# A long convolution beside a gated MLP on one core: the inverse transform's turn on VectorE in place of a trip through DRAM, with a new written order

## The chip, the cores and the metric

The kernel runs on one core of one Trainium2 chip. The metric is the device time in microseconds (us) of one execution; lower is better. Times of several runs are given as a median with the lowest and the highest. The profile is that of one more execution, whose own time and span are given beside the median.

## The reference: what is computed

With `xn = layernorm(A_q)` over 640 columns and 2048 rows, the output is the sum of three parts:

```python
kv  = causal_4_tap_filter(A_k, A_shift_k) * A_v          # per column, along the rows
y   = irfft(rfft(kv, 4096) * rfft(A_ssm_k, 4096))[:2048] # a long causal convolution per column
A   = xn * (bf16(y) + kv * A_ssm_D)
h   = sigmoid(xn @ B_w_gate) * (xn @ B_w_up)             # 640 -> 1728
B   = h @ B_w_down                                       # 1728 -> 640
out = A_q + A + B
```

All inputs and the output are bf16.

## The kernel before, in words

**Layout.** Row 16p + b of the sequence lies on partition p, block b (16 blocks). `x` and `xn` are [128, 16, 640] tiles in SBUF; the results are added into `x`, which is stored at the end.

**The MLP** goes in four row tiles t of 512 rows (four blocks each). `gate_mm` and `up_mm` (both through `product`, L293) make one 128-wide slice of the hidden layer with five matmuls each; ScalarE takes the sigmoid (`gate_ev`, L302) and VectorE multiplies (`up_ev`, L308). `down_mm` (L334), `pair_mm` (L341) and `rest_mm` (L351) go back to 640 columns and VectorE adds the sums into `x` (`down_ev` L345, `rest_ev` L356).

**The convolution** goes in five chunks c of 128 columns. Each is a transform in two steps, a product, and an inverse in two steps:

- `kv_op` (16 letters `k` for each chunk; L384 to L393, VectorE): the four taps and the product with v. `h_turn` (`H`, L370, VectorE) turns the filter by 32x32 transposes; it reads with a step of 32 bytes and writes densely.
- `st1_mm` (`a`, L409 and L411, TensorE): the first step, a sum over the 128 partitions. `st1_ev` (`A`, or `I` when VectorE copies it instead of ScalarE) evicts it to the tile `t1`; `wr1` (`w`, L423) writes `t1` to a DRAM buffer and `rd2` (`r`, L433) reads it back in another order.
- `st2_mm` (`b`, L443), `st2_ev` (`B`, or `F` for VectorE), `prod` (`p`: a shuffle at L456 and a product at L458, VectorE).
- `inv1_mm` (`c`, L472), twice for each chunk (y = 2c and 2c+1). Its output has, on each quarter of 32 partitions, 32 indices (h, b), and along the free dimension 16 indices r times 128 columns. `inv1_ev` (`C` on ScalarE, L256, or `J` on VectorE, L259; two 128x1024 halves for each y) evicts it to the tile `ao`.
- **The turn.** The second inverse step needs r on the partitions and (h, b) along the free dimension. In the kernel before, `wr2` (`W`, L488 or L492) writes `ao` to the DRAM buffer `d2`, and two `rdb` (`R`, L502) for each chunk read it back as `bi` in the other order. These DMAs are issued by SyncE (SP), each behind whatever SP waits for ahead of it.
- `inv2_mm` (`d`, L511), `inv2_q` (`q`, L516: times `xn`) and `inv2_x` (every other `q`, L521: into `x`).

In the profile all copies by ScalarE stand at L256 and all copies by VectorE at L259; the tile's name tells them apart (`t`, `xz`, `ao`, `kx`). Some of `ao` and `bi` lie in the `kx` tiles once those are free.

**The order.** Each engine runs its instructions in the order in which the program lists them. That order is written out by hand as `ORDER`, a string of 824 letters; each letter takes the next step of its chain. `F`, `J` and `I` take a step of `B`, `C` and `A` with VectorE as the copying engine. `TURNS` permutes two of the chains: `m`, the loads at the start, and `o`, the stores at the end. TensorE has psum tiles in two pools: `psC` (two buffers of two banks, for the transforms) and `psG` (four, for the MLP and the second inverse step).

**Stores.** `store` (L359) sends 14 pieces: 512 columns of one or two row blocks, or the last 128 columns of one to four row blocks. SP issues them, except the very last, which ScalarE issues.

Of the kernel before, what the change touches and what calls it, by code (L numbers as in the profile page):

```python
# [10 lines left out]
BF16 = mybir.dt.bfloat16  # L11
F32 = mybir.dt.float32
# [5 lines left out]
DM = 640  # L18
FF = 1728
P = 128  # L20
NB = S // P
NC = DM // P
NFC = 14
NQ = 4
# [13 lines left out]
def _tables():  # L38

    p = np.arange(P)
    k1 = p + 0.25
    s1 = np.zeros((P, NB, 2, P))
    for b in range(NB):
        psi = 2 * np.pi * k1[None, :] * (16 * p + b)[:, None] / 2048.0
        s1[:, b, 0, :] = np.cos(psi)
        s1[:, b, 1, :] = -np.sin(psi)
    tb = s1.transpose(3, 2, 1, 0) / 2048.0  # L50
    th = 2 * np.pi * np.outer(np.arange(NB), np.arange(NB)) / 16.0
    c, s = np.cos(th), np.sin(th)
# [13 lines left out]
def kernel(  # L66
# [14 lines left out]
    nc = tc.nc  # L81
# [3 lines left out]
    outr = out.flatten_outer_dims().rearrange("(p b) d -> p b d", b=NB)  # L85
# [26 lines left out]
    TB = TBt.bitcast(BF16)  # L112
# [3 lines left out]
    x = res.tile([P, NB, DM], BF16, name="x")  # L116
# [16 lines left out]
    sync = nc.sync  # L133
# [222 lines left out]
        nc.vector.tensor_tensor(xs, pds[t, b0][:, b0:b1, :], xs, ALU.add)  # L356

    def store(b0, b1, lo, hi):
        (nc.scalar if b1 == NB and hi == DM else sync).dma_start(outr[:, b0:b1, lo:hi], x[:, b0:b1, lo:hi])  # L359


    def add_D(c):
# [49 lines left out]

    def st1_ev(c, n, copy=act_copy):
        d = chunks[c]
        if n % 2 == 0:
            d[n // 2] = cv.tile([P, 8, 2, P], BF16, name="t1", bufs=2)
        o = 4 * (n % 2)
        copy(out=d[n // 2][:, o:o + 4, :, :].rearrange("p b s c -> p s b c"), in_=pss[n][:, :, :, :])

    def wr1(c, k):  # L420
        h, part = divmod(k, 2)
        d = chunks[c]
        sync.dma_start(d["d1"][:, h, 8 * part:8 * part + 8, :], d[k].rearrange("p b s c -> p b (s c)"))  # L423

    groups = {}
    xz = cv.tile([P, 3, 3, 8, P], BF16, name="xz")
# [34 lines left out]
    def inv1_mm(y):  # L461

        c, y2 = divmod(y, 2)
        d = chunks[c]
        if y2 == 0:
            d["d2"] = dr.tile([32, P, P], BF16, name="d2", bufs=NC)
        d["pa", y] = ps = [psC.tile([P, 2, 512], F32, name="psa", tag="c") for _ in range(2)]
        lo, hi = sorted((2 * y % 3, (2 * y + 1) % 3))
        for i in range(2):
            for q in range(NQ):  # L470
                for g in range(4):
                    nc.tensor.matmul(ps[g // 2][quad(q), g % 2, :], lhsT=SM[quad(g), i, :],  # L472
                                     rhs=xz[quad(g), lo:hi + 1:hi - lo, 1 + i, 2 * q:2 * q + 2, :],
                                     start=(i == 0), stop=(i == 1))

    def inv1_ev(y, n, copy=act_copy):
        d = chunks[y // 2]
        if n == 0:
            d["ao", y] = kxs[1][:, 0:NB, :] if y >= 7 and y % 2 else cv.tile([P, 16, P], BF16, name="ao")[:, :, :]
        dst = d["ao", y].rearrange("p (s g e) c -> p g s (e c)", s=2, g=4)  # L480
        copy(out=dst[:, 2 * n:2 * n + 2, :, :],
                       in_=d["pa", y][n].rearrange("p g (s f) -> p g s f", s=2))

    def wr2(y):
        c, y2 = divmod(y, 2)
        d = chunks[c]
        if 2 * y % 3 < 2:
            sync.dma_start(d["d2"][16 * y2:16 * y2 + 16].rearrange("r p c -> p r c"), d["ao", y])  # L488
            return
        for n in range(2):  # L490
            lo = 16 * y2 + 8 - 8 * n
            sync.dma_start(d["d2"][lo:lo + 8].rearrange("r p c -> p r c"), d["ao", y][:, 8 * n:8 * n + 8, :])  # L492

    def rdb(c, n):

        d = chunks[c]
        if c >= 3 and n == 1:
            bi = kxs[0][:, 0:NB, :].rearrange("p (h b) c -> p h b c", h=2)
        else:
            bi = cv.tile([P, 2, 8, P], BF16, name="bi")[:, :, :, :]  # L500
        src = d["d2"].rearrange("r (q h b) c -> (r q) h (b c)", q=NQ, h=2)
        sync.dma_start(bi.rearrange("p h b c -> p h (b c)"), src[:, :, 1024 * n:1024 * n + 1024])  # L502
        d["bi", n] = bi

    def inv2_mm(c, m):

        bi = chunks[c]["bi", m // 2]
        chunks[c]["pb", m] = ps = psG.tile([P, 4, P], F32, name="psb", tag="g")
        for i in range(4):
            for h in range(2):  # L510
                nc.tensor.matmul(ps[:, i, :], lhsT=TB[:, h, 4 * m + i, :], rhs=bi[:, h, 4 * (m % 2) + i, :],  # L511
                                 start=(h == 0), stop=(h == 1))

    def inv2_q(c, m):
# [63 lines left out]
    def step(k, fn, *args):  # L578
        chains[k].append((fn, args))
# [62 lines left out]
    for c in range(NC):  # L642
        for n in range(2):
            step("H", h_turn, c, n)
        step("D", add_D, c)
        for n in range(8):
            step("a", st1_mm, c, n)
            step("A", st1_ev, c, n)
        for n in range(4):
            step("w", wr1, c, n)  # L650
        for s in range(4 * c, 4 * c + 4):
            step("r", rd2, s)
            step("b", st2_mm, s)
# [9 lines left out]
        for n in range(2):  # L663
# [28 lines left out]
    for b in (0, 4, 8, 12):  # L692
# [2 lines left out]
    step("o", store, NB - 1, NB, 4 * P, DM)  # L695

    ORDER = """
    mmmmgggmssggmuLuLmsggsZgmugmgmLsuuggsmgggsmkLkgkkkumsmgkusmmgkPgmullmlgulHmgsusgmHmuggDgggmkksuskkaA
    kkkanggkkHaTAAegKuHeawmtkegkkekLgugaAuAgkkaADLgguaawAukmgsgAkggTuLksakkkkkggsguuwLPAkmkaAsthgggsKaaH
    HwVAAugukggaamwsskKKrukkkwkkAAklgggauADkksVggTbwlguBgakssglBkkkAuspprgbBgguBkasnkaKKwIggthTuaAkaugAI  # L700
    suggawspHuLLklkVkkAkkawApggakaLsgkkAKkgeemgAceLPuuggrgHuuCCbBrekkwgVFgkgppDlkkaAauKAggwhsulbgtgBBrwk
    suHaAaAggpsbBBpuWgsgkkwVgucggksrpprCCaaWIAsggukalusaIggukAbFggsuBpbBHsgggpugsswDFcunkpKkCRpkrgCrgsaw
    aIguuAdqdbFqVBppggsWbrggBBqlcCpuJksggbqBuBkgpgrsbBggkkkkkuBaaIgeeuppRdqqepaewAdWArwaAgRaarugAIggqwuc
    CggJswqbpBFupggsdqbBpguWqrrBpdqgscCJqugugbFBgppsuRgbBpggsuddqWqBrrscCJRgugbqqppBBWspggsrbrBBggupupdd
    RqcJgsCpgsubFBprggsbBBuggpsqqudcCdgqJbquWpRRBBpggWsgsppuugcCgJdqqqqgqddqgdqqWogqqsggguguRdRuqooodqqq
    qoggudoogoqqodguoqouoqoo
# [38 lines left out]
```

## Time and profile before

| | before |
|---|---|
| median of 3 runs | 236.81 us (236.79 to 237.27) |
| the profiled execution's own time | 238.36 us |
| its span in the trace | 236.5 us |
| TensorE busy | 227.2 us |
| VectorE busy | 202.1 us |
| ScalarE busy | 134.7 us |
| DMA moved | 56.13 MB |

The span runs from the first to the last event of the trace. Busy times are the union of an engine's instructions; TensorE's matmuls are pipelined and their ends are modelled, so a TensorE that is shown as busy can still lose a little between matmuls. A row "a <- b: 5.0, 2, 3.1" of the view of waits says that the engine stood still before a for 5.0 us in all, two times, at most 3.1 us, until b was done.

### The profile page before, as it was taken

How to read it: one execution, taken by the hardware profiler on the slowest of the kernel's cores; microseconds unless marked ns; L12 is line 12 of the kernel's file. 1: busy time of each engine (PE TensorE's matmuls, PEld its weight loads, DVE VectorE, ACT ScalarE, POOL GpSimd, SP SyncE). 2: the span in 40 equal slices, each digit the busy share in tenths (PEclk: the TensorE clock that was granted, in tenths of full speed). 3: DMA queues.
4: the chain of work that ended last, by engine and by line, in shares of the span. 5: the costliest groups of instructions: out<-in, count | busy, mean ns of one | idle time of the engine just before them, and what ended most of it. 6: DMA issues, size and time to landing. Idle time of an engine off the chain costs nothing.

```text
span 236.5 us, 5598 instructions
## 1 busy us (share of the span) xinstructions
PE 227.2 (96%) x2281; PEld 112.0 (47%) x2281; DVE 202.1 (85%) x321; ACT 134.7 (57%) x197; POOL 12.1 (5%) x27
## 2 busy tenths in 40 slices
PE   8999999979999999999999999999999999999990
PEld 2854444436444444447444445445654444445480
DVE  5542983899898989999998999999999999999591
ACT  2458521368886686993976566566365684651000
POOL 4210020000040000020000000000000000000000
PEclk9999999999999999999999999999999999999998
DMA  6999997997999997799999996899999885684775
GB/s 181 305 264 267 256 306 180 236 230 209 231 274 276 301 238 208 140 226 306 282 245 255 298 333 138 219 242 257 247 288 269 224 237 176 173 247 110 222 242 160
DMA packets 98223, 56.13 MB, mean 237 GB/s; under 512 B 56342, under 2 KB 92438, under 8 KB 98070
## 3 DMA queue, kind: packets, MB, share of 16 engines
q1 hardware_dynamic: 97622, 55.42, 89.3%
q8 instruction: 18, 0.29, 0.5%
q10 hardware_dynamic: 576, 0.36, 0.5%
q14 instruction: 7, 0.06, 0.1%
HBM read 35.45 MB, written 18.35 MB: 228 GB/s over the span
## 4 chain that ended last, share of the span: by engine, by line
PE 63%; DVE 15%; SPq 9%; DMA 8%; issue 3%; DVEq 0%
PE pg L293 16%; PE pu L293 16%; PE pd L334 13%; PE pr L351 4%; DMA kx<-in_A_k_dram 4%; PE ps L409 4%; PE ps L411 4%; DMA w<-in_B_w_up_dram 3%; DVE yx L516 3%; PE ps L443 2%; PE psa L472 2%; SPq L185 2%; DVE x L521 2%; SPq L188 2%; DVE xz L458 2%
## 5 line engine op out<-in xcount | busy, mean ns | idle before, releaser
L293 PEld LDWEIGHTS <-w 128*128 128x128 bf16 x500 | 47.0, 98 | 58.1 <-issue 4.8
L293 PE MATMUL pu<-xnT,w 128*128 128x512 bf16 x250 | 62.3, 380 | 0.0
L293 PE MATMUL pg<-xnT,w 128*128 128x512 bf16 x250 | 62.2, 379 | 0.0
L334 PE MATMUL pd<-wd,hT 128*128 128x512 bf16 x208 | 48.4, 379 | 0.3 <-DMA wd<-in_B_w_down_dram 0.2
L308 DVE TENSOR_TENSOR hT<-sig,pu 128x512 bf16<-128x512 bf16 x52 | 35.0, 682 | 12.5 <-PE pu L293 6.8
L302 ACT ACTIVATE sig<-pg 128x512 bf16<-128x512 f32 x52 | 30.9, 601 | 23.8 <-PE pg L293 20.3
L256 ACT CAST xz<-ps 128x1024 bf16<-128x1024 f32 x33 | 32.4, 1017 | 16.8 <-PE ps L443 16.8
L256 ACT CAST t<-ps 128x1024 bf16<-128x1024 f32 x33 | 32.5, 1011 | 16.6 <-PE ps L411 14.7
L334 PEld LDWEIGHTS <-hT 128*128 128x128 bf16 x208 | 19.7, 98 | 24.9 <-issue 2.7
L458 DVE TENSOR_TENSOR xz<-xz 128x2048 bf16<-128x2048 bf16 x20 | 24.4, 1220 | 0.3
L390 DVE TENSOR_TENSOR acc<-acc,tmp 128x1024 bf16<-128x1024 bf16 x30 | 20.7, 689 | 0.6
L388 DVE TENSOR_TENSOR tmp<-kx,sc 128x1024 bf16<-128x1024 bf16 x30 | 20.7, 689 | 0.5
L409 PE MATMUL ps<-kvh,S1t 128*128 128x512 bf16 x40 | 15.2, 379 | 1.2 <-DVE kvh L393 1.2
L411 PE MATMUL ps<-kvh,S1t 128*128 128x512 bf16 x40 | 15.5, 387 | 0.0
L456 DVE STREAM_SHUFFLE xz<-xz 128x512 f32<-128x512 f32 x20 | 14.5, 725 | 0.0
L516 DVE TENSOR_TENSOR yx<-psb,xn 128x512 bf16<-128x512 f32 x20 | 13.7, 685 | 0.7
L351 PE MATMUL pr<-wd,hT 128*128 128x128 bf16 x224 | 14.2, 219 | 0.0
L351 PEld LDWEIGHTS <-hT 128*128 128x128 bf16 x224 | 13.1, 98 | 2.0 <-issue 0.6
L256 ACT CAST ao<-psa 128x1024 bf16<-128x1024 f32 x11 | 10.8, 1013 | 4.0 <-PE psa L472 2.6
L345 DVE TENSOR_TENSOR x<-pd,x 128x512 bf16<-128x512 f32 x16 | 10.6, 683 | 2.9 <-PE pd L341 2.3
L511 PEld LDWEIGHTS <-TBt 128*128 128x128 bf16 x160 | 10.1, 98 | 3.6 <-issue 0.7
L370 DVE STREAM_TRANSPOSE kvh<-hn 128x512 f32<-128x512 f32 x10 | 10.9, 1096 | 0.0
(62 smaller groups left out, 189.3 us busy)
## 6 DMA issues: line engine op xcount, KB each, us to landing
d<-t SPq DMA_DIRECT2D x20, 512.0 KB, 5.2
t<-d SPq DMA_DIRECT2D x20, 512.0 KB, 5.3
bi<-d SPq DMA_DIRECT2D x8, 512.0 KB, 8.6
d<-ao SPq DMA_DIRECT2D x6, 512.0 KB, 5.3
kx<-in_A_k_dram SPq DMA_DIRECT2D x10, 256.0 KB, 5.2
kvh<-in_A_v_dram SPq DMA_DIRECT2D x10, 256.0 KB, 5.4
hn<-in_A_ssm_k_dram SPq DMA_DIRECT2D x20, 128.0 KB, 5.8
x<-in_A_q_dram SPq DMA_DIRECT2D x3, 640.0 KB, 5.4
```

Of the source, the lines that this page charges most:

```text
L256: nc.scalar.copy(out=out, in_=in_)
L293: nc.tensor.matmul(pg[:, :], lhsT=w[:, c, u * UP + fc * P:u * UP + (fc + 1) * P], rhs=xnT[:, :, c, :], start=(c == 0), stop=(c == NC - 1))
L302: nc.scalar.activation(sig[fc][:, :], pgs[0, fc][:, :], ACT.Sigmoid)
L308: nc.vector.tensor_tensor(hT[:, fc, :], sig[fc][:, :], pgs[1, fc][:, :], ALU.mult)
L334: nc.tensor.matmul(pds[bb][:, :], lhsT=hT[:, fc, bb * P:(bb + 1) * P], rhs=wd[:, fc, 0:4 * P], start=(fc == 0), stop=(bb > 1 and fc == NFC ...
L351: nc.tensor.matmul(pds[t, b0][:, bb, :], lhsT=hT[:, fc, bb * P:(bb + 1) * P], rhs=wd[:, fc, 4 * P:DM], start=(fc == 0), stop=(fc == NFC - 1))
L388: nc.vector.tensor_tensor(d["tmp"][:, :, :], kx[:, lo + 3 - m:hi + 3 - m, :], sb(m), ALU.mult)
L390: nc.vector.tensor_tensor(d["acc"][:, :, :], d["acc"][:, :, :], d["tmp"][:, :, :], ALU.add)
L409: nc.tensor.matmul(ps[:, 0, :, :], lhsT=S1[:, h, :], rhs=cin[c]["kvh"][:, 0, 4 * n4:4 * n4 + 4, :], start=True, stop=True)
L411: nc.tensor.matmul(ps[:, 1, :, :], lhsT=S1[:, h, :], rhs=hp[:, 2 * n4:2 * n4 + 2, :, :], start=True, stop=True)
L458: nc.vector.tensor_tensor(z[:, 1:3, :, :], z[:, 0:1, :, :].to_broadcast((P, 2, 8, P)), z[:, 1:3, :, :], ALU.mult)
L516: nc.vector.tensor_tensor(yx[:, :, :], chunks[c]["pb", m][:, :, :], xn[:, 4 * m:4 * m + 4, c * P:(c + 1) * P], ALU.mult)
```

## The change

Four things change together.

1. **The turn.** `wr2`, `rdb` and the buffer `d2` go. Both y of a chunk are evicted to one `ao` of 32 rows by 128 columns, seen as 64 pairs of bf16 (float32). Four `inv_turn` for each chunk (letter `R`, now on VectorE), each over 16 of the 64 pairs, transpose it in place in 32x32 blocks. `inv2_mm` reads `ao` itself. The table `TB` has its rows reordered to fit. For chunk 3 `ao` is the tile `t1`, for chunk 4 the `kx` tiles, which are now one tile.
2. **Who copies.** Of the letters that copy by VectorE, `F` goes from 7 to 3, `I` from 7 to 3 and `J` from 7 to 4; these eleven evictions go to ScalarE.
3. **The order.** `ORDER` and `TURNS` are new throughout. Letters `g`, `s`, `u`, `k`, `H`, `p`, `q` and so on are as many as before. `W` (10) is gone, and `R` is 20 instead of 10.
4. **Stores.** Those of the last 128 columns for row blocks 8 to 11 and 12 to 14 are issued by ScalarE too.

```diff
-    tb = s1.transpose(3, 2, 1, 0) / 2048.0
+    tb = (s1.transpose(3, 2, 1, 0) / 2048.0).reshape(32, NQ, 2, NB, P).transpose(1, 0, 2, 3, 4).reshape(P, 2, NB, P)
...
-    kxs = [res.tile([P, NB + 3, P], BF16, name="kx%d" % i) for i in range(2)]
+    kx2 = res.tile([P, 2, NB + 3, P], BF16, name="kx2")
+    kxs = [kx2[:, i, :, :] for i in range(2)]
+    t1 = res.tile([P, 2, 8, 2, P], BF16, name="t1")
...
-        (nc.scalar if b1 == NB and hi == DM else sync).dma_start(outr[:, b0:b1, lo:hi], x[:, b0:b1, lo:hi])
+        (nc.scalar if b1 > 11 and hi == DM else sync).dma_start(outr[:, b0:b1, lo:hi], x[:, b0:b1, lo:hi])
...
-        if n == 0:
-            d["ao", y] = kxs[1][:, 0:NB, :] if y >= 7 and y % 2 else cv.tile([P, 16, P], BF16, name="ao")[:, :, :]
-        dst = d["ao", y].rearrange("p (s g e) c -> p g s (e c)", s=2, g=4)
+        if n == 0 and y % 2 == 0:
+            if y // 2 < 3:
+                d["ao"] = cv.tile([P, 32, P], BF16, name="ao")[:, :, :]
+            elif y // 2 == 3:
+                d["ao"] = t1.rearrange("p i b s c -> p (i b s) c")
+            else:
+                d["ao"] = kx2.rearrange("p i b c -> p (i b) c")[:, 0:32, :]
+        dst = d["ao"][:, 16 * (y % 2):16 * (y % 2) + 16, :].rearrange("p (s g e) c -> p g s (e c)", s=2, g=4)
...
-    def wr2(y):
...
-    def rdb(c, n):
...
+    def inv_turn(c, n):
+
+        a = chunks[c]["ao"].bitcast(F32).rearrange("p r c -> p c r")[:, 16 * n:16 * n + 16, :]
+        nc.vector.transpose(a, a)
...
-        bi = chunks[c]["bi", m // 2]
+        bi = chunks[c]["ao"].rearrange("p (h b) c -> p h b c", h=2)
...
-            step("W", wr2, y)
-        for n in range(2):
-            step("R", rdb, c, n)
+        for n in range(4):
+            step("R", inv_turn, c, n)
...
-    TURNS = {"m": [0, 1, 21, 7, 2, 23, 9, 4, 5, 15, 6, 10, 18, 12, 13, 14, 8, 22, 17, 11, 20, 16, 25, 24, 26, 19, 3],
-        "o": [3, 6, 1, 7, 4, 5, 2, 9, 10, 8, 0, 12, 11, 13]}
+    TURNS = {"m": [2, 1, 4, 10, 0, 9, 21, 7, 5, 6, 11, 14, 15, 12, 13, 8, 18, 20, 16, 17, 22, 23, 24, 25, 26, 19, 3],
+        "o": [2, 0, 4, 1, 5, 3, 6, 8, 9, 10, 7, 11, 12, 13]}
```

The written order is read off the two strings by counting letters. What the prediction uses:

| letter number in `ORDER` | before | after |
|---|---|---|
| `k` number 1, 8, 9, 16 (chunk 0's taps) | 44, 92, 93, 109 | 12, 64, 72, 96 |
| first and last `R` | 490, 791 | 437, 790 |
| last `p`, last `c`, last `C` or `J` | 755, 759, 762 | 766, 769, 785 |
| first `o` and fifth `o` (stores) | 778, 802 | 758, 778 |

The start of the new string, for the loads: `mZmgsmgugsmkgummgggkkmLsummgggsusLugsmLLmmm...`; its end: `...sooCqggggCRRRqRgoguuoduqgqdqdgodqqgoqoqqouoguoguoo`. In the new `TURNS`, the loads `m` begin with chunk 0's taps, a `w_up` slice, a `w_gate` slice, the first half of chunk 0's k, the `w_gate` slice that came first before, and chunk 0's halo; the second half of chunk 0's k is 11th instead of 20th.

More of the change, by code (lines that the diff above doesn't have):

```diff
@@ L414, in st1_ev @@
         d = chunks[c]
-        if n % 2 == 0:
-            d[n // 2] = cv.tile([P, 8, 2, P], BF16, name="t1", bufs=2)
         o = 4 * (n % 2)
-        copy(out=d[n // 2][:, o:o + 4, :, :].rearrange("p b s c -> p s b c"), in_=pss[n][:, :, :, :])
+        copy(out=t1[:, n // 2 % 2, o:o + 4, :, :].rearrange("p b s c -> p s b c"), in_=pss[n][:, :, :, :])
     def wr1(c, k):
@@ L422, in wr1 @@
         d = chunks[c]
-        sync.dma_start(d["d1"][:, h, 8 * part:8 * part + 8, :], d[k].rearrange("p b s c -> p b (s c)"))
+        sync.dma_start(d["d1"][:, h, 8 * part:8 * part + 8, :], t1[:, k % 2, :, :, :].rearrange("p b s c -> p b (s c)"))
     groups = {}
@@ L464, in inv1_mm @@
         d = chunks[c]
-        if y2 == 0:
-            d["d2"] = dr.tile([32, P, P], BF16, name="d2", bufs=NC)
         d["pa", y] = ps = [psC.tile([P, 2, 512], F32, name="psa", tag="c") for _ in range(2)]
@@ L477, in inv1_ev @@
         d = chunks[y // 2]
-        if n == 0:
-            d["ao", y] = kxs[1][:, 0:NB, :] if y >= 7 and y % 2 else cv.tile([P, 16, P], BF16, name="ao")[:, :, :]
-        dst = d["ao", y].rearrange("p (s g e) c -> p g s (e c)", s=2, g=4)
+        if n == 0 and y % 2 == 0:
[6 more added lines that the diff above has]
+        dst = d["ao"][:, 16 * (y % 2):16 * (y % 2) + 16, :].rearrange("p (s g e) c -> p g s (e c)", s=2, g=4)
         copy(out=dst[:, 2 * n:2 * n + 2, :, :],
                        in_=d["pa", y][n].rearrange("p g (s f) -> p g s f", s=2))
-    def wr2(y):
[L485 to L489, printed above, removed]
-        for n in range(2):
-            lo = 16 * y2 + 8 - 8 * n
-            sync.dma_start(d["d2"][lo:lo + 8].rearrange("r p c -> p r c"), d["ao", y][:, 8 * n:8 * n + 8, :])
-    def rdb(c, n):
[L496 to L503, printed above, removed]
+    def inv_turn(c, n):
+        a = chunks[c]["ao"].bitcast(F32).rearrange("p r c -> p c r")[:, 16 * n:16 * n + 16, :]
+        nc.vector.transpose(a, a)
     def inv2_mm(c, m):
-        bi = chunks[c]["bi", m // 2]
+        bi = chunks[c]["ao"].rearrange("p (h b) c -> p h b c", h=2)
         chunks[c]["pb", m] = ps = psG.tile([P, 4, P], F32, name="psb", tag="g")
@@ L510, in inv2_mm @@
             for h in range(2):
-                nc.tensor.matmul(ps[:, i, :], lhsT=TB[:, h, 4 * m + i, :], rhs=bi[:, h, 4 * (m % 2) + i, :],
+                nc.tensor.matmul(ps[:, i, :], lhsT=TB[:, h, 4 * m + i, :], rhs=bi[:, h, 4 * m + i, :],
                                  start=(h == 0), stop=(h == 1))
@@ L661 @@
                 step("C", inv1_ev, y, n)
-            step("W", wr2, y)
-        for n in range(2):
-            step("R", rdb, c, n)
+        for n in range(4):
+            step("R", inv_turn, c, n)
         for m in range(4):
@@ L697 @@
     ORDER = """
[L698 to L706, printed above, removed]
-    """
-    TURNS = {"m": [0, 1, 21, 7, 2, 23, 9, 4, 5, 15, 6, 10, 18, 12, 13, 14, 8, 22, 17, 11, 20, 16, 25, 24, 26, 19, 3],
-        "o": [3, 6, 1, 7, 4, 5, 2, 9, 10, 8, 0, 12, 11, 13]}
+    mZmgsmgugsmkgummgggkkmLsummgggsusLugsmLLmmmkkggkuggHHsmmkmmsggmkmPuusDmkggggskkkmukgugsmkkalAHakggsA
+    TnmuuaaIltgggglkkksgkkALLlkaawAeuLgAgkmeakwkggukgkkuueeDKagAaTumAggggaLwkkHtsAsAggKkkuakwKgPuahVKskI
+    kugsugAgwmkkaskgrgsAugaAgsgbBTHkBkKVkgwkkkruukwkslggkptaulAaggkknkKVsukksKAwDaArgsakkgAwLHguubggBFss
+    kkaIahgAugwLaTAappgaAukrgkLmasAAkkkgkukegbBwpggeLFVsllHKcCgpHuuteepCgwDaggArubBuBgkkkkkkggkkpaagAAgh
+    usbBBwuggVpHsHapgAaagguAApcssggurCJkRKsuaggkuwawrDAkRkRARaAsggnukkbBBsgpgsubBgrrwudpaqBdddAcqqCCpqqV
+    pggsqubBBqPgsgpbgBBgqspcCCwgrgkruubBBsgsgkkbgBBRrRRRduauplqsdulpAqqraAwgeaAlggaqpppdaeqqdqAAgscCgJbB
+    eggqlFpppbggBBercCuugguuwCrgaAggbrpRsBBRRRggsuugbBgpppBgwsgcusuCJggsppbBdqrduqgguqBprbqspgdqquBBggsc
+    dCppggqrCbsuuggBRRBgRsusbggBRdpsqupgqqdqgBcgCJgsuupprbggqoBsuBpggpodcsudqqosooCqggggCRRRqRgoguuoduqg
+    qdqdgodqqgoqoqqouoguguoo
+    """
+    TURNS = {"m": [2, 1, 4, 10, 0, 9, 21, 7, 5, 6, 11, 14, 15, 12, 13, 8, 18, 20, 16, 17, 22, 23, 24, 25, 26, 19, 3],
+        "o": [2, 0, 4, 1, 5, 3, 6, 8, 9, 10, 7, 11, 12, 13]}
     left = {k: iter([v[i] for i in TURNS.get(k, range(len(v)))]) for k, v in chains.items()}
```

## The prediction

> **What bounds the kernel now.** I read the page first: span, busy times, the slices.
>
> ```profile
> span 236.5 us, 5598 instructions
> ...
> PE 227.2 (96%) x2281; PEld 112.0 (47%) x2281; DVE 202.1 (85%) x321; ACT 134.7 (57%) x197; POOL 12.1 (5%) x27
> ...
> DMA  6999997997999997799999996899999885684775
> ...
> DMA packets 98223, 56.13 MB, mean 237 GB/s; under 512 B 56342, under 2 KB 92438, under 8 KB 98070
> ```
>
> TensorE is busy nearly always, VectorE 85% of the time, and the DMA engines are nearly full. An average does not say who sets the end, so next come the busy times in stretches of 20 us (columns: stretch, then PE, PEld, DVE, ACT, POOL, clock, DMA share, GB/s).
>
> ```profile
> 0.00:20.00 20.00, 18.82 (x148) 10.98 (x149) 8.93 (x25) 10.02 (x19) 4.93 (x16) 1.00 0.97 253
> 20.00:40.00 20.00, 20.00 (x94) 9.11 (x93) 14.65 (x23) 8.67 (x18) 2.16 (x3) 1.00 1.09 263
> 40.00:60.00 20.00, 18.60 (x129) 9.55 (x128) 16.51 (x25) 12.21 (x19) 0.42 (x1) 1.00 0.91 217
> ...
> 100.00:120.00 20.00, 20.00 (x256) 10.17 (x254) 19.73 (x31) 15.40 (x22) 2.02 (x4) 1.00 1.02 257
> ...
> 160.00:180.00 20.00, 20.00 (x278) 11.19 (x275) 19.39 (x32) 10.85 (x13) 0.00 (x0) 1.00 0.95 266
> ...
> 200.00:220.00 20.00, 19.63 (x244) 9.79 (x243) 19.10 (x31) 8.69 (x12) 0.00 (x0) 1.00 0.64 172
> 220.00:237.00 17.00, 10.37 (x115) 6.98 (x112) 8.19 (x16) 0.00 (x0) 0.00 (x0) 0.95 0.67 201
> ```
>
> From 100 us to 220 us VectorE has 19.1 to 19.7 us of every 20. It is as full as TensorE there, and the free time it has lies before 60 us and after 220 us. So an edit that gives VectorE more work is paid for unless that early and late time is used. The third view is the list of waits (total, times, longest).
>
> ```profile
> DVE hT L308 <- PE pu L293: 6.8, 7, 1.5
> ...
> DVE hT L308 <- ACT sig L302: 5.3, 2, 2.6
> ...
> DVE acc L384 <- DMA kx<-in_A_k_dram: 4.2, 1, 4.2
> ...
> DVE x L345 <- PE pd L341: 2.3, 1, 2.3
> ...
> PE idle L539 <- DVE hT L129: 1.2, 1, 1.2
> ...
> PE psb L511 <- DVE yx L516: 0.2, 1, 0.2
> ```
>
> The last row is the only one with `psb`, the second inverse step, and it names VectorE, not `bi`: no engine stands still for the trip through DRAM. It is hidden already. Taking it away shortens no wait that the profile shows; it frees room in the order and on the queue.
>
> **The change part by part.**
>
> *What goes: the trip.* The listing of DMA issues has it:
>
> ```profile
> bi<-d SPq DMA_DIRECT2D x8, 512.0 KB, 8.6
> d<-ao SPq DMA_DIRECT2D x6, 512.0 KB, 5.3
> ...
> d<-ao SPq DMA_DIRECT2D x4, 256.0 KB, 3.7
> ...
> kx<-d SPq DMA_DIRECT2D x2, 512.0 KB, 6.1
> ...
> d<-kx SPq DMA_DIRECT2D x2, 256.0 KB, 4.7
> ...
> d<-kx SPq DMA_DIRECT2D x1, 512.0 KB, 3.8
> ```
>
> Writes: 6 x 512 + 4 x 256 + 2 x 256 + 512 = 5120 KB; reads: 10 x 512 = 5120 KB. That is 10.5 of 56.1 MB, and 23 issues on SP. I cost its going at nothing: other work hid it. What it buys is distance: 5.3 us out and 8.6 us back stood between the last eviction of a chunk and its second step; now it is four turns.
>
> *What comes: 20 turns.* The trace of before has no transpose that writes with a step. The nearest rows:
>
> ```profile
> L456 DVE STREAM_SHUFFLE xz<-xz 128x512 f32<-128x512 f32 x20 | 14.5, 725 | 0.0
> ...
> L370 DVE STREAM_TRANSPOSE kvh<-hn 128x512 f32<-128x512 f32 x10 | 10.9, 1096 | 0.0
> ```
>
> `inv_turn` has the same 128x512 float32 as `h_turn` at L370, 1096 ns, which reads with a step of 32 bytes and writes densely. The new one reads and writes with a step of 256 bytes. Low end: 725 ns, the shuffle of as many elements, dense on both sides. High end: if the 371 ns between these two rows are the price of the stepped reads, and stepped writes cost the same on top, 1467 ns. I take 1096, the same operation, and keep both ends. What counts on a full engine is the distance to the next start:
>
> ```profile
> 67.23 2.10 DVE L370 STREAM_TRANSPOSE kvh<-hn 128x512 f32<-128x512 f32 x2
> 69.26 1.24 DVE L308 TENSOR_TENSOR hT<-sig,pu 128x512 bf16<-128x512 bf16 x2
> ...
> 187.44 1.22 DVE L259 CAST ao<-psa 128x1024 bf16<-128x1024 f32 x1
> 188.58 0.68 DVE L308 TENSOR_TENSOR hT<-sig,pu 128x512 bf16<-128x512 bf16 x1
> ```
>
> Two turns take 69.26 - 67.23 = 2.03 us, 1.015 each, and an eviction by VectorE 1.14 us. So: 20 x 1.015 = 20.3 us come.
>
> The Trainium skill speaks against this edit: "SBUF — State Buffer", in the section on Door 1, says that SBUF has lines of 16 bytes and that each access which crosses to a new line pays a penalty. Here every element of the turn crosses, in reading and in writing; by that page both sides would pay, which is the first rival below. The 1096 beside 725 ns agrees for reads; no run here shows it for writes.
>
> *What moves to ScalarE: eleven evictions* (4 + 4 + 3). VectorE is rid of 11 x 1.14 = 12.5 us. ScalarE gets 11 x 1.01 us by this row:
>
> ```profile
> L256 ACT CAST ao<-psa 128x1024 bf16<-128x1024 f32 x11 | 10.8, 1013 | 4.0 <-PE psa L472 2.6
> ```
>
> That makes 146 us busy of some 235, so it costs nothing as long as nobody waits behind one; if the cover is gone it costs VectorE the waits of rival 2.
>
> VectorE's balance: +20.3 - 12.5 = **+7.8 us**.
>
> *What the order gives back.* Stops of VectorE early and late, and its last instruction:
>
> ```profile
> 12.48 1.28 DVE L308 TENSOR_TENSOR hT<-sig,pu 128x512 bf16<-128x512 bf16 x2 [2.64 <-ACT sig L302]
> ...
> 23.55 0.69 DVE L308 TENSOR_TENSOR hT<-sig,pu 128x512 bf16<-128x512 bf16 x1 [1.47 <-PE pu L293]
> ...
> 41.99 0.69 DVE L384 TENSOR_TENSOR acc<-kx,sc 128x1024 bf16<-128x1024 bf16 x1 [4.20 <-DMA kx<-in_A_k_dram]
> ...
> 222.57 1.29 DVE L345 TENSOR_TENSOR x<-pd,x 128x512 bf16<-128x512 f32 x2 [2.33 <-PE pd L341]
> ...
> 230.81 0.43 DVE L521 TENSOR_TENSOR x<-x,yx 128x512 bf16<-128x512 bf16 x1
> ```
>
> - The 4.2 us stop at 42 us is for the second half of chunk 0's k, the 20th of the loads; it becomes the 11th, and the ninth `k` comes at letter 72. I take all 4.2 us as gone. Between none and 4.2.
> - `up_ev` waits 6.8 + 5.3 us, most of it from 9.8 to 23.6 us, while nothing else lies in VectorE's queue: the first `k` of before is letter 44. It is letter 12 now, and the first half of k is the fourth load. The first 2.6 us stay (no `k` ahead of it); of the other 9.5 I take 4.0 as filled, about six `kv_op`. Bounds: none and 9.5. In exchange one gate slice lands after k; TensorE, without a stop there now, may lose up to 1 us, which I leave in the range.
> - The stop of 2.3 us at 220 us waits for TensorE. With VectorE the fuller engine at the end, TensorE will be ahead: gone.
>
> Given back: 4.2 + 4.0 + 2.3 = 10.5 us.
>
> *New waits.* A turn must wait for the last `inv1_ev` of its chunk. For chunk 4 the last `C` is the letter right before the first `R`: `prod`, then `inv1_mm`, then two ScalarE evictions of 1.01 us, with about 1.5 us of VectorE work beside them. I put 1.3 us there; behind the waiting turn stand the last `u` and `q`, the whole end. 0.7 us for the other four chunks, whose `R` stand at least five letters behind their last `C`. Reuse of `ao`, `t1` and `kx`: nothing, since the last `wr1` of a half of `t1` is issued tens of letters ahead.
>
> VectorE's last instruction ends at 231.24 + 7.8 - 10.5 + 2.0 = **230.5 us**.
>
> *The end: stores.*
>
> ```profile
> SPq L359 <- DVE x L521: 9.1, 2, 5.4
> ...
> SPq L740 <- DMA out_dram<-x: 2.2, 1, 2.2
> ...
> SPq L740 <- PEq L740: 0.6, 2, 0.4
> ...
> 231.27 0.35 ACTq L359 DMA_DIRECT2D out_dram<-x  x1
> ...
> out_dram<-x SPq DMA_DIRECT2D x1, 96.0 KB, 2.6
> ```
>
> After 231.24 before needs 5.25 us more: SP was held 5.4 us by one `inv2_x` and then sent nearly all stores in a heap, and the last data came late. Now the fifth store is letter 778, not 802, so five 256 KB stores leave over 10 us ahead of the end, and ScalarE, idle then, issues three. The least that remains is an issue of 0.35, a landing of 2.6 and the closing, 0.6 us of waits and, as an estimate, 0.3 us around them: 3.9 us. Between 3.9 and 5.3; I take 3.9.
>
> Sum: span 230.5 + 3.9 = 234.4 us. The profiled execution took 238.36 by its own clock for a span of 236.5; the median of 236.81 is 0.3 above that span, so **234.7 us**, 0.9% below before.
>
> **The rivals.**
>
> 1. *The turn pays for stepped writes (slower).* For it: 1096 beside 725 ns, and a step of 256 bytes on both sides. Against it: reads and writes may overlap. Price: 20 x 0.371 = 7.4 us on the engine that is full: 242.1 us. It decides early: the forecast's gain of 2.1 us is used up at 0.105 us a turn, so from 1.2 us a turn on the change is no gain. Chance 0.24; a turn dearer still (1.9 us gives 250) another 0.07.
> 2. *VectorE waits for ScalarE at every turn.* The eleven evictions now lie in ScalarE's queue behind sigmoids, and VectorE is in order. Four more stops of 1.3 us: 239.9 us. Against it: ScalarE still has some 90 us idle. Chance 0.11.
> 3. *The early time isn't filled*, because k lands no sooner than VectorE frees anyway (the DMA share is 0.97 to 1.09 up to 40 us): 234.7 + 4.0 = 238.7 us. Chance 0.06.
> 4. *The turn is cheap* (725 ns): VectorE gets 7.4 us back and TensorE sets the end: 1.2 + 227.2, 0.9 for VectorE behind it and 3.9 make 233.2; modelled ends may hide some 2 us: 231. Chance 0.07.
>
> That the trip goes but nothing comes of it is contained in the forecast: it counts zero for it.
>
> **How the numbers follow.** Forecast 0.45, for itself 232 to 237.5. Range: 231.0 (rival 4) to 243.0 (rival 1 with one more us of waits); outside lie the dearest turn and little of the others, under 0.2. A measurement of this kernel tells about 0.2% from no change, 236.34 to 237.28. Faster: 0.37 of the forecast, 0.07 of rival 4, 0.03 of rivals 2 and 3: 0.47. Same: 0.05 + 0.02 = 0.07. Slower: 0.31 of rival 1, 0.12 of 2 and 3, 0.03 of the forecast: 0.46.
>
> **What would show it.** The row of the turn: 1.1 us carries the forecast, 1.47 rival 1. VectorE's busy time should be near 210 us, ScalarE's near 146, DMA 45.6 MB. No stop for `kx` at the taps; the first `kv_op` before 20 us; VectorE's last instruction near 230.5 and the span 4 us behind it. Wrong would be: waits of VectorE on `ao`, or TensorE waiting for `w` before 35 us.

## The result, and the profile after

| | before | after |
|---|---|---|
| median on the same chip | 236.96 us (236.65 to 240.34, 7 runs) | 236.04 us (235.9 to 236.11, 7 runs) |
| ratio | | 0.9959, 95% interval 0.9947 to 0.9972 |
| the profiled execution's own time | 238.36 us | 236.04 us |
| its span | 236.5 us | 234.1 us |

The change is worth 0.9 us, 0.4%. The forecast was a gain of 2.1 us. The page of after, first three parts:

```profile
span 234.1 us, 5562 instructions
...
PE 226.4 (97%) x2270; PEld 111.6 (48%) x2281; DVE 209.9 (90%) x330; ACT 145.1 (62%) x208; POOL 11.8 (5%) x27
...
DMA  6999999997999996999878396354275350202524
...
DMA packets 74815, 45.65 MB, mean 195 GB/s; under 512 B 35494, under 2 KB 71590, under 8 KB 74662
```

VectorE has 7.8 us more work, ScalarE 10.4 us more, and the DMA engines 10.5 MB less: the second half of the DMA row (tenths of a slice) was mostly eights and nines and is now mostly 5 or less. Next the busy times of after in stretches (PE, PEld, DVE, ACT, POOL, clock, DMA share, GB/s):

```profile
20.00:40.00 20.00, 19.95 (x93) 9.09 (x93) 17.59 (x27) 11.41 (x24) 2.86 (x4) 1.00 1.11 272
...
100.00:120.00 20.00, 19.16 (x220) 9.88 (x220) 19.71 (x30) 14.95 (x20) 1.50 (x4) 1.00 1.03 239
160.00:180.00 20.00, 19.58 (x317) 9.92 (x317) 19.49 (x29) 11.91 (x14) 0.00 (x0) 1.00 0.46 134
200.00:220.00 20.00, 19.89 (x232) 9.44 (x233) 19.04 (x29) 9.86 (x14) 0.00 (x0) 1.00 0.24 80
```

From 20 to 40 us VectorE now does 17.59 us of work where it did 14.65. Later TensorE and VectorE are both full, as before; at 200 us the DMA share is down from 0.64 to 0.24. VectorE's waits in after:

```profile
DVE hT L310 <- PE pu L295: 4.1, 4, 1.5
DVE hT L310 <- ACT sig L304: 3.6, 2, 2.6
...
DVE t L261 <- PE ps L413: 1.8, 2, 1.4
DVE acc L386 <- ACT sc L165: 1.0, 1, 1.0
DVE xz L456 <- PE psa L470: 0.9, 1, 0.9
...
DVE kx L490 <- ACT kx L258: 0.6, 1, 0.6
DVE acc L386 <- DMA kx<-in_A_k_dram: 0.5, 1, 0.5
DVE ao L490 <- ACT ao L258: 0.3, 1, 0.3
```

The two rows for `hT` were 6.8 and 5.3, the stop for k was 4.2, and the turns (L490) wait for ScalarE less than 1 us in all. So the body did much of what it was to do. The end is where the time shows. VectorE's last two instructions in after:

```profile
230.41 0.68 DVE L347 TENSOR_TENSOR x<-pd,x 128x512 bf16<-128x512 f32 x1
231.01 0.28 DVE L358 TENSOR_TENSOR x<-pr,x 128x128 bf16<-128x128 f32 x1
```

They end at 231.29 us, no earlier than the profiled execution of before (231.24), but the span ends 2.8 us later instead of 5.3. The reason is in the stretch behind it. The busy times of before from 232 to 234 us:

```profile
232.00:234.00 2.00, 0.00 (x0) 0.00 (x0) 0.00 (x0) 0.00 (x0) 0.00 (x0) 1.00 0.98 288
```

The same stretch of after:

```profile
232.00:234.00 2.00, 0.00 (x0) 0.00 (x0) 0.00 (x0) 0.00 (x0) 0.00 (x0) 1.00 0.25 79
```

In before the DMA engines still work at 0.98 of their time when all computing is over; in after at 0.25. The stores of before leave SP in one heap, so their data arrives late (timeline of SP's issues in before: start, us, count):

```profile
225.37 7.83 SPq L359 DMA_DIRECT2D out_dram<-x  x12
```

In after SP issues eleven stores, from 212.5 us on:

```profile
212.50 18.96 SPq L361 DMA_DIRECT2D out_dram<-x  x11
```

### The profile page after: what moved, and what is told of

Its sections match the earlier page's. It is cut to its first block, busy times and chain, and to the rows that moved or that the text cites. A ratio compares the mean times of both kernels' runs of the same rounds, so it can differ in the third digit from the quotient of the medians.

```text
span 234.1 us, 5562 instructions
## 1 busy us (share of the span) xinstructions
PE 226.4 (97%) x2270; PEld 111.6 (48%) x2281; DVE 209.9 (90%) x330; ACT 145.1 (62%) x208; POOL 11.8 (5%) x27
## 4 chain that ended last, share of the span: by engine, by line
PE 25%; DVE 24%; issue 3%; DVEq 0%
PE pu L295 6%; PE pg L295 6%; PE pd L336 6%; DVE ao L490 3%; DVE yx L503 3%; DVE hT L310 3%; DVE xz L458 3%; DVE xz L456 2%; PE psb L498 2%; DVE x L508 2%; DVE tmp L390 2%; PE ps L443 1%; PE pr L353 1%; PE psa L470 1%; DVE acc L392 1%
## 5 line engine op out<-in xcount | busy, mean ns | idle before, releaser
L336 PE MATMUL pd<-wd,hT 128*128 128x512 bf16 x198 | 46.3, 379 | 0.8 <-issue 0.5
L258 ACT CAST t<-ps 128x1024 bf16<-128x1024 f32 x37 | 36.6, 1012 | 14.9 <-PE ps L413 13.5
L258 ACT CAST xz<-ps 128x1024 bf16<-128x1024 f32 x37 | 36.0, 1019 | 12.2 <-PE ps L443 12.2
L310 DVE TENSOR_TENSOR hT<-sig,pu 128x512 bf16<-128x512 bf16 x52 | 34.4, 678 | 8.1 <-PE pu L295 4.1
L390 DVE TENSOR_TENSOR tmp<-kx,sc 128x1024 bf16<-128x1024 bf16 x30 | 20.6, 687 | 0.5
L490 DVE STREAM_TRANSPOSE ao<-ao 128x512 f32<-128x512 f32 x12 | 13.7, 1202 | 0.3 <-ACT ao L258 0.3
L258 ACT CAST ao<-psa 128x1024 bf16<-128x1024 f32 x10 | 9.8, 1014 | 4.2 <-PE psa L470 4.1
L498 PEld LDWEIGHTS <-TBt 128*128 128x128 bf16 x160 | 9.9, 98 | 4.3 <-issue 1.2
```

The costliest lines, as they stand in the source:

```text
L258: nc.scalar.copy(out=out, in_=in_)
L310: nc.vector.tensor_tensor(hT[:, fc, :], sig[fc][:, :], pgs[1, fc][:, :], ALU.mult)
L336: nc.tensor.matmul(pds[bb][:, :], lhsT=hT[:, fc, bb * P:(bb + 1) * P], rhs=wd[:, fc, 0:4 * P], start=(fc == 0), stop=(bb > 1 and fc == NFC ...
L390: nc.vector.tensor_tensor(d["tmp"][:, :, :], kx[:, lo + 3 - m:hi + 3 - m, :], sb(m), ALU.mult)
L490: nc.vector.transpose(a, a)
```

## The experiments

Three theories stood against each other. **A**: VectorE is the bound of the body, so its account (turns, evictions, filled waits) carries the gain. **C**, formed after the first four runs: the gain is the end alone, and the body is held by TensorE, or by TensorE and VectorE tied together. **D**: the late second half of k in the old loads is what makes the times of before scatter, and costs it part of its median. **B** is the rival of each run. Every run lay beside runs of before on its chip, and ratios are to those. Where a run is set beside after's 236.04 us, the two did not run side by side; the lowest times of before in the several groups of runs lie between 236.65 and 236.82 us.

### Before once more

No edit.

> The kernel before, unchanged, profiled once more. Its first profiled execution took 238.36 us with a span of 236.5 us, while its median is 236.81 to 236.96 us. Theory A: that execution was itself about 1.5 us slower than usual, and the time around a span is 1.9 us, as in the changed kernel (236.04 for 234.1): this one takes about 236.9 us with a span near 235.0, and the 1.5 us are missing in a place that can be named (the stop for k at 42 us, or the end behind VectorE's last instruction). Rival B: a profile always adds 1.5 us to this kernel: 238.4 and 236.5 again.

Measured: 237.14 us, span 235.3. From VectorE's waits in this run:

```profile
DVE acc L384 <- DMA kx<-in_A_k_dram: 2.1, 1, 2.1
```

The timeline of the same run:

```profile
229.41 0.43 DVE L521 TENSOR_TENSOR x<-x,yx 128x512 bf16<-128x512 bf16 x1
```

The stop for k is 2.1 us, not 4.2, and VectorE is done at 229.84, not 231.24. The profiled execution of before that the prediction was built on was 1.2 us longer than a usual one. This matters for all that follows: against this execution the *body* of after ends 1.45 us later, and only the end makes up for it. It also shows that a time is its span and 1.8 us more: 237.14 - 235.3; likewise 238.36 - 236.5 = 1.9, and 236.04 - 234.1 = 1.9 in after.

### The turn's price, in four views

The four turns of a chunk read and write in all four ways; three of them leave the data in other places than the reference needs, so the output is another.

```diff
-        nc.vector.transpose(a, a)
+        f = chunks[c]["ao"].bitcast(F32).rearrange("p (n r) c -> p n (r c)", n=4)[:, n, :].rearrange("p (a b) -> p a b", b=32)
+        if n == 0:
+            nc.vector.transpose(a, a)
+        elif n == 1:
+            nc.vector.transpose(f, a)
+        elif n == 2:
+            nc.vector.transpose(a, f)
+        else:
+            nc.vector.transpose(f, f)
```

> In the changed kernel the four turns of a chunk differ: the first reads and writes with the step of 256 bytes, the second reads so and writes densely, the third reads densely and writes so, the fourth is dense on both sides (the last three move wrong elements). Theory A: the steps cost, reads most: about 1.20, 1.10, 0.85 and 0.75 us. Rival B: a transpose of 512 float32 takes 1.1 us whatever its steps, and only the stepped write adds: 1.20, 1.10, 1.20, 1.10. Time by A about 1 to 3 us under the changed kernel's 236.0, by B under 1 us.

Measured: 235.55 us (one time). The groups by form, L492 with both sides stepped, L494 with stepped reads alone, L496 with stepped writes alone, L498 dense (the last figure before the second bar is the mean in ns):

```profile
L492 DVE STREAM_TRANSPOSE ao<-ao 128x512 f32<-128x512 f32 x3 | 3.7, 1222 | 0.3 <-ACT ao L258 0.3
L496 DVE STREAM_TRANSPOSE ao<-ao 128x512 f32<-128x512 f32 x3 | 3.2, 1075 | 0.1
L494 DVE STREAM_TRANSPOSE ao<-ao 128x512 f32<-128x512 f32 x3 | 3.2, 1070 | 0.1
L498 DVE STREAM_TRANSPOSE ao<-ao 128x512 f32<-128x512 f32 x3 | 2.1, 711 | 0.1
```

Stepped writes alone cost as much as stepped reads alone, 0.36 us over the dense form; both together cost 0.51, not 0.72. Theory A had the reads right and the writes too cheap; rival B fell, since the dense form takes 0.71 us and not 1.10. The time, of one run, is 0.5 us below after's 236.04, not the 1 to 3 us of theory A, with 2.2 us less work on VectorE (207.7 against 209.9).

### Without the turns

`inv_turn` does nothing: the second inverse step reads data that was not turned.

```diff
-        nc.vector.transpose(a, a)
+        return
```

> The changed kernel without the 20 turns, so the second inverse step reads data that was never turned; the rest stays. VectorE has 22 us less. Theory A (VectorE is the bound from 30 us to the end): TensorE takes over and the time falls to 231 to 233 us. Rival B (the turns lie in time in which VectorE would wait for TensorE anyway): 235 to 236 us.

Measured: 235.24 us (234.9 to 235.33), ratio 0.9896 (0.9834 to 0.9958). The busy times of this run:

```profile
PE 225.2 (97%) x2270; PEld 111.5 (48%) x2281; DVE 189.3 (81%) x310; ACT 145.3 (62%) x208; POOL 11.7 (5%) x27
```

Its waits of VectorE:

```profile
DVE hT L310 <- ACT sig L304: 10.8, 6, 2.9
...
DVE hT L310 <- PE pu L295: 7.4, 7, 2.0
...
DVE x L347 <- PE pd L343: 4.7, 1, 4.7
```

20.6 us of VectorE's work are gone, and the kernel is 0.8 us shorter. The waits for the MLP's `hT` go from 7.7 to 18.2 us, and one of 4.7 us for `pd` comes: VectorE waits for TensorE and what TensorE feeds. **Theory A falls here**: VectorE is nearly full, but its work alone does not set the time. The order stayed the one that was written for the turns.

### Late stores back to SP

```diff
-        (nc.scalar if b1 > 11 and hi == DM else sync).dma_start(...)
+        (nc.scalar if b1 == NB and hi == DM else sync).dma_start(...)
```

> The changed kernel with two of its three late ScalarE stores given back to SyncE. Theory A (VectorE's last instruction and the short end set the time, ScalarE's part is small): 236.0 to 236.6 us. Rival B (the whole gain is the stores by ScalarE): 236.9 to 237.2 us, as before the change.

Measured: 236.19 us (235.85 to 237.43, 12 runs), ratio 0.9946 (0.9919 to 0.9974). VectorE's last instruction ends 2.9 us before the span. ScalarE's part of the stores does nothing that can be told. That leaves the early letters `o`; no run took these back in the changed kernel, so there it is argued, and the next runs test both in the kernel before.

### ScalarE's stores in the kernel before

The counterpart: the kernel before with the change's store rule alone.

```diff
-        (nc.scalar if b1 == NB and hi == DM else sync).dma_start(...)
+        (nc.scalar if b1 > 11 and hi == DM else sync).dma_start(...)
```

> The kernel before with only part 4 of the change: the stores of the last 128 columns for row blocks 8 to 11 and 12 to 14 are issued by ScalarE. Theory C says that the end of before is long because twelve stores leave together from 224 us on, behind one that waits, and that who issues the last two or three matters little: 236.7 to 237.1 us, no change beyond 0.3 us, with over 4.5 us from VectorE's last instruction to the end. Rival: ScalarE's late stores alone shorten the end: 235 to 235.6 us.

Measured: 237.19 us (236.69 to 238.21, 12 runs), ratio 0.9995 (0.9974 to 1.0016): no difference. SP's waits in this run:

```profile
SPq L359 <- DVE x L521: 9.1, 2, 5.4
```

SP's timeline:

```profile
224.00 7.30 SPq L359 DMA_DIRECT2D out_dram<-x  x10
```

Two issues are off SP, but SP still stands 5.4 us before an `inv2_x` and then sends ten stores in a heap. The end stays at 5.1 us (229.86 to 235.0).

### Early stores in the kernel before

The kernel before with its old turn; only the stores move. Six letters `o` go up to letter 782, behind the last `s`, and ScalarE issues the pieces that are ready there.

```diff
-        (nc.scalar if b1 == NB and hi == DM else sync).dma_start(...)
+        (nc.scalar if hi == 4 * P and b1 <= 12 or b1 == NB and hi == DM else sync).dma_start(...)
...
-        "o": [3, 6, 1, 7, 4, 5, 2, 9, 10, 8, 0, 12, 11, 13]}
+        "o": [0, 1, 2, 3, 4, 5, 6, 7, 9, 10, 8, 12, 11, 13]}
```

> The kernel before, turn through DRAM and all, with only the stores changed: the six stores of 512 columns for row blocks 0 to 11 are issued by ScalarE after its last sigmoid work, in the order of their rows, and no longer by SyncE behind one for blocks 12 and 13. Theory C (the change's whole gain is the end: 5.3 to 5.5 us from VectorE's last instruction to the end of the span before, 2.8 after): the end falls to about 3 us, and the time to 234.6 to 235.6 us, below the changed kernel's 236.0. Theory A (VectorE's time given back carries the gain): 236.5 to 237.0 us, as before.

Measured: 235.18 us (234.68 to 238.82, 7 runs), ratio 0.9911 (0.9879 to 0.9943). With the old trip through DRAM and none of the turns this is, by the ratio, 2.1 us below the runs of before beside it (median 237.63 us), and 0.9 us below the median of after. In its profiled execution, the 238.82 us one, the end is 3.2 us (233.81 to 237.0). It supports C: the whole gain can be had from the stores. The interval of the ratio lies below that of after, 0.9947 to 0.9972; the two kernels did not run side by side, so their distance is less sure than either ratio.

### Half of the second inverse step

TensorE's work is cut: only half of the sum over (h, r) is formed.

```diff
-            for h in range(2):
+            for h in range(1):
...
-                                 start=(h == 0), stop=(h == 1))
+                                 start=(h == 0), stop=(h == 0))
```

> The changed kernel without the second half of the sum in the second inverse step: 80 of its 160 matmuls are left out, 4.5 us of TensorE; VectorE does all that it did. Theory A (VectorE is the bound): 235.5 to 236.0 us. Theory C (TensorE is the bound of the body, as the run without turns says): 232 to 234 us.

Measured: 234.92 us (234.79 to 234.98), ratio 0.9891 (0.9863 to 0.9919). TensorE's busy time is 223.4 us, 3.0 less than in after; the time is 1.1 us less. The 3.0 is a lower bound: 11 of 2281 matmuls are missing from the trace of after and none from this one. The rows of this step itself add up to 11.5 us in after and 7.2 here.

### Half of that step, and no turns

Both edits together.

> Both left out: half of the second inverse step and all turns. If one engine alone were the bound, this would be no better than leaving out its work alone. If the two are tied to each other, each has no slack behind the other and only leaving out both pays: theory C says 230.5 to 232 us, theory A (VectorE alone) 235.2 us as without turns.

Measured: 232.71 us (232.62 to 233.23), ratio 0.9804 (0.9775 to 0.9832). The busy times of this run:

```profile
PE 222.4 (96%) x2201; PEld 107.2 (46%) x2201; DVE 189.2 (82%) x310; ACT 145.0 (63%) x208; POOL 11.7 (5%) x27
```

One alone gives 0.8, the other alone 1.1, both 3.3 us, more than their sum of 1.9. That is what two engines look like that hold each other: freed of one, the kernel soon meets the other. These are differences of medians; by the ratios they are 1.5, 1.6 and 3.7 us, so that both together give more than either is sure, and that they give more than the sum is less so. C's direction held in both runs; its ranges (232 to 234, and 230.5 to 232) were too low, by 0.9 and 0.7 us at their upper ends.

### Eleven evictions back to VectorE

In after, four `B` become `F`, four `A` become `I`, three `C` become `J`, evenly spread over the part of the string behind letter 250. The places are not planned ones.

> The changed kernel with eleven evictions given back to VectorE at evenly spread places (7 F, 7 I, 7 J, as before): 12.5 us more on VectorE, 11 us less on ScalarE. With its turns VectorE then has some 222 us of 236. Theory C with both engines tied: VectorE becomes the bound and the time rises by 2 to 6 us, to 238 to 242 us. Rival (VectorE's load counts for little, as leaving out the turns gave only 0.8 us): 236 to 236.5 us.

Measured: 250.15 us (249.83 to 252.02), ratio 1.0555 (1.0521 to 1.059). The busy times of this run:

```profile
PE 231.0 (92%) x2281; PEld 113.7 (45%) x2281; DVE 222.2 (89%) x341; ACT 135.7 (54%) x197; POOL 11.8 (5%) x27
```

VectorE's busy time grows by 12.3 us and the time by 14.1. Taking 20.6 us off VectorE gave 0.8; putting 12.3 us on it costs all of that and more. Part of it is the places: in the profiled execution (252.02 us) VectorE also stands idle 3.7 us longer than in after before its last instruction, 3.4 of them in one wait of an eviction for TensorE. So the change could not have carried the turns with the old division of the evictions, in places like these. That is more than was expected.

### The new order with the old turn

The kernel before with the new `ORDER`, `TURNS` and stores; `W` behind every second `C` or `J` of a y, one `R` of a chunk at its first turn's place and one behind its second `d`.

```diff
-    ORDER = <before>
+    ORDER = <after, with W put in and two R for each chunk in place of four>
```

> The new order, loads, evictions by ScalarE and stores, with the old turn through DRAM: a write behind each second eviction of a y, the first read in place of the first turn, the second behind the second product of the chunk. VectorE has 22 us less than in the changed kernel, and the trip of some 10 us stands in an order that was not made for it. Theory C (TensorE bounds the body, VectorE's 22 us are worth 0.8 us): 235 to 238 us, by how long TensorE waits for the trip. Theory A (the turn on VectorE costs about what it adds): 231 to 234 us.

Measured: 289.52 us (286.97 to 290.56), ratio 1.2218 (1.2174 to 1.2261). TensorE's waits in this run:

```profile
PE ps L443 <- DMA t<-d: 20.1, 5, 7.7
PE psb L511 <- DMA bi<-d: 10.5, 3, 5.6
PE ps L409 <- ACT t L256: 9.5, 1, 9.5
```

TensorE stands 20.1 us before the second step of the *forward* transform, whose data (`t<-d`) comes through the same SP queue, 10.5 us before `bi`, and 9.5 us for a psum buffer that ScalarE had still to empty. Its mean granted clock was 0.94 in this execution, where it is 1.00 in after. Both theories' ranges (231 to 238 us) were far off. So the trip that no engine waited for in the old order is far from free in the new one, with `W` and `R` where I put them; other places were not tried. It also means that this run does not tell what the new order is worth without the turn, which was its purpose.

### The loads of k exchanged

The kernel before; the second half of chunk 0's k goes from 20th to sixth among the loads, and the load that was sixth (`m` 23) takes its place.

```diff
-        "m": [0, 1, 21, 7, 2, 23, 9, ... 22, 17, 11, 20, ...
+        "m": [0, 1, 21, 7, 2, 11, 9, ... 22, 17, 23, 20, ...
```

> The kernel before with two loads of 256 KB exchanged in the list of first loads: the second half of chunk 0's k becomes the sixth, the first half of chunk 1's k the twentieth. Theory D: the late and uneven landing of that half is what spreads the times of before (236.7 to 240.9 us): TensorE waits behind VectorE at 42 to 50 us, and where it waits longer its clock falls for some microseconds. Then these runs lie within 0.5 us of each other, near the fast runs of before: 236.2 to 236.8 us, with no stop for k and a granted clock of 1.0 from 44 to 56 us. Rival: the spread comes from the trip through DRAM or the stores, and stays.

Measured: 237.02 us (236.66 to 237.2, 12 runs), ratio 0.999 (0.9979 to 1.0002). The stop for `kx` is gone from the waits, but the median is the same as that of before beside it (237.1), above the 236.2 to 236.8 of theory D: D is wrong on the median. What VectorE got back it waits for elsewhere. This row was 2.8 us in before_again:

```profile
DVE x L345 <- PE pd L341: 4.5, 3, 2.3
```

So in the kernel before, too, 2.1 us of VectorE's idle time were worth nothing: TensorE was no sooner ready. On the scatter the run points D's way without showing it: the times lie within 0.54 us, those of before beside it within 1.24 (236.65 to 237.89, 17 runs); the 240 us that before reached beside other runs did not come up here.

### Both edits to the kernel before

`swap_k` and the early stores together.

> The kernel before, turn through DRAM kept, with the two loads exchanged and the early stores. Theories C and D together: 234.3 to 234.9 us, runs within 0.5 us, so faster than the kernel before and than the changed one (236.0). If the changed kernel's gain needed the turn on VectorE: 236 us or more.

Measured: 235.05 us (234.77 to 235.69, 6 runs), ratio 0.99 (0.9882 to 0.9917), the shortest median of all that compute the whole of the reference, though not to be told from the 235.18 of the early stores alone, and with the old turn. It is just above the 234.3 to 234.9 of theories C and D, and below the 236 us at which the gain would have needed the turn on VectorE; the runs lie within 0.9 us, not 0.5. VectorE's last instruction in its timeline:

```profile
230.18 0.43 DVE L521 TENSOR_TENSOR x<-x,yx 128x512 bf16<-128x512 bf16 x1
```

The stores that ScalarE issues:

```profile
216.33 14.71 ACTq L359 DMA_DIRECT2D out_dram<-x  x7
```

Those of SP:

```profile
224.74 6.26 SPq L359 DMA_DIRECT2D out_dram<-x  x7
```

Seven stores begin to leave ScalarE at 216 us, while SP still serves the trip. VectorE is done at 230.61, and the span of 233.8 ends 3.2 us later: an end 0.4 us longer than after's, behind a body 0.7 us shorter. This execution, of 235.69 us, is the longest of the six.

## Why the prediction was wrong, point by point

The direction was right and the range held the time; the size, 2.1 us, was more than twice the 0.9 measured.

**The step that failed is the last one:** "the median of 236.81 is 0.3 above that span, so 234.7". The span came out near, 234.4 against 234.1, by luck: VectorE's last instruction came 0.8 us later than forecast and the end was 1.1 us shorter. But a time is its span and 1.8 to 1.9 us, as the profiled execution itself had it (238.36 and 236.5). Setting the span of one execution beside the median of others gave 0.3, since that execution was 1.2 us longer than a usual one, in its span and its time alike. With its own distance of 1.9 the same sum ends at 236.3 us, 0.2% below before. So 1.6 of the 2.1 us forecast were no gain of the change, but the distance between that execution and a usual one. In the sum it shows at the stop for k: 4.2 us to be given back in that execution, 2.1 in the other. Worked on that other execution, with its 2.1, the account gives 229.84 + 7.8 - 8.4 + 2.0 = 231.2 us for VectorE's last instruction (measured 231.29), and with the forecast's own end of 3.9 and 1.8 around the span 236.9 us: nearly no gain.

**VectorE's account was nearly right in sum**, with single terms off both ways.

| term | forecast | measured |
|---|---|---|
| a turn: its row, its distance to the next start | 1.096, 1.015 us | 1.202, 1.10 us |
| 20 turns | 20.3 us | 22 us by distance; 20.6 us of busy time, by leaving them out |
| VectorE busy | 210 us | 209.9 us |
| early `up_ev` waits filled | 4.0 us | 4.4 us (12.1 to 7.7) |
| stop for k given back | 4.2 us | 0.6 us of the usual 2.1: 0.5 stays, 1.0 is new at `sc` |
| tail wait given back | 2.3 us | gone, but for 0.2 us |
| waits of the turns | 2.0 us | 0.9 us; waits of `xz` and `t` for `psa` grew from 0.2 to 1.6 |
| VectorE's last instruction | 230.5 us | 231.29 us |
| from there to the end | 3.9 us | 2.8 us |

The turn's row in the groups of after:

```profile
L490 DVE STREAM_TRANSPOSE ao<-ao 128x512 f32<-128x512 f32 x12 | 13.7, 1202 | 0.3 <-ACT ao L258 0.3
```

The distance between turns is read in the timeline, four of them from 173.16 to 177.56, 4.40 us:

```profile
173.16 4.49 DVE L490 STREAM_TRANSPOSE ao<-ao 128x512 f32<-128x512 f32 x4 [0.30 <-ACT ao L258]
177.56 0.64 DVE L358 TENSOR_TENSOR x<-pr,x 128x512 bf16<-128x512 f32 x1
```

The first `kv_op` stands at 15.52 us, before the 20 us named, in the timeline of after:

```profile
15.52 0.68 DVE L386 TENSOR_TENSOR acc<-kx,sc 128x1024 bf16<-128x1024 bf16 x1
```

No wait of TensorE for `w` and hardly one of VectorE on `ao` is in the waits of after, which I had named as signs against it. Idle time of VectorE up to its last instruction is 231.29 - 209.9 = 21.4 us, against 229.84 - 202.1 = 27.7 in the second execution of before: 6.3 us of waits filled and 7.8 us of work added, so the body ends 1.45 us later.

**The reason behind it was wrong.** I took VectorE for the engine that sets the end and let each of its microseconds count. Without the turns 20.6 us of its work save 0.8 us. TensorE, "busy nearly always" in my first view, holds the body as much; the balance came out near the truth because what VectorE got and what it lost were nearly equal, which is luck. Two readings would have warned me. VectorE was not "as full as TensorE" from 100 to 220 us: in the stretch from 120 to 140 us, which I did not show, it has 18.70 us and TensorE 20.00. And the page has the chain that ended last, in shares of the span by engine. On the page of before:

```profile
PE 63%; DVE 15%; SPq 9%; DMA 8%; issue 3%; DVEq 0%
```

On that of before_again, the usual execution:

```profile
PE 80%; DVE 12%; issue 3%; DMA 2%; SPq 1%; DVEq 0%
```

On that of after, where the chain is followed back only to 108 us:

```profile
PE 25%; DVE 24%; issue 3%; DVEq 0%
```

By this chain TensorE held most of the body of before, and in the part of after that it covers the two have equal shares. As I had it, each microsecond more or less would have moved the time by one. Downward it did not hold; upward 12.3 us more cost 14.1, in one run with unplanned places.

**The end was undersized.** Of the terms that shorten the time it is the only one that survives: 5.3 or 5.45 us become 2.8, a gain of 2.5, where I took 1.4. I named its cause rightly (the heap of stores behind one `inv2_x`), but gave part of it to ScalarE's issuing, which is worth nothing that can be told, alone or taken back.

**The rivals.** Rival 1 (stepped writes) has a real mechanism: they cost 0.36 us alone. But with stepped reads they add only 0.15 and the row came out at 1.20, just at the turning point of 1.2 that I had named for it, far from 1.47. Rival 2 (waits at each turn) fell: 0.9 us in all. Rival 3 (early time not filled) fell: 4.4 us of the `up_ev` waits were filled, though little of the stop for k. Rival 4 is half true: the turn is not cheap, but TensorE does hold the body, and without any turn the kernel, in this order, still takes 235.2 us, not 231.

**Open.** Against a usual execution of before the body of no_turn still ends 0.4 us later (230.25 and 229.84), with 12.8 us less work on VectorE. Whether the new order or its psum buffers cost that was not told apart.

## What to carry to other kernels

Before you price an edit, set the profiled execution's own time beside the median. Where it is longer, as it was by 1.5 us here, what you work out from it may be a gain over that execution only. Read the chain that ended last before you call an engine the bound. Two engines that are both about 90% busy or more can be tied to each other, as here: test each by leaving work out before you count its microseconds. Here removing gave little and adding cost its full price. Look at the DMA share after the last computing instruction; where it is near 1, as the 0.98 of before, try moving the stores that are ready forward: here that gained 2.1 us with only the stores changed.

## What the runs showed of the hardware that I had not expected

A 32x32 transpose of 128x512 float32 took 0.71 us dense, 1.07 with a step of 256 bytes on the reads or on the writes alone, and 1.22 with both. The Trainium skill, "SBUF — State Buffer", in the section on Door 1, has a penalty for each access that crosses to a new line of 16 bytes; that agrees for reads and for writes one at a time. By adding the two penalties the turn would take 1.43 us; the trace has 1.22, so both together cost less than their sum. Why was not tested.

TensorE's granted clock fell after a short wait. In the profiled execution of before_early_stores, the longest of its runs, k came late and TensorE waited for the filter's product; its timeline has:

```profile
49.31 0.39 PE L409 MATMUL ps<-kvh,S1t 128*128 128x512 bf16 x1 [1.83 <-DVE kvh L393]
...
51.01 4.27 PE L334 MATMUL pd<-wd,hT 128*128 128x512 bf16 x12
```

Its busy times in two stretches:

```profile
48.00:52.00 4.00, 2.69 (x11) 0.88 (x12) 3.94 (x6) 2.02 (x3) 0.42 (x1) 0.83 0.98 238
...
51.00:54.00 3.00, 3.00 (x9) 1.03 (x8) 2.93 (x5) 2.97 (x6) 0.00 (x0) 0.50 1.12 197
```

TensorE was busy 2.69 us of the first 4. From 51 to 54 us, after the wait, it was busy all the time at a clock of 0.50, and twelve matmuls took 4.27 us; in the profiled execution of before (its timeline), where the wait at the same place was 1.22 us and the clock stayed at 1.00, the same twelve take 2.75:

```profile
50.09 2.75 PE L334 MATMUL pd<-wd,hT 128*128 128x512 bf16 x12
```

So in this execution a wait of 1.83 us on a late load cost TensorE 1.5 us more behind it. Whether this makes the scatter of before was not shown: swap_k, whose loads leave no such wait, has the narrower spread, but before beside it had none of the longest times either.
